# Attention and two feed-forward layers on one core: keys split before they are transposed, GpSimd's long subtractions in parts, column sums as two more columns, weights decoded in place, reciprocals taken through DRAM

## The chip, the cores and the metric

The kernel runs on one core of one Trainium2 chip. The metric is the device time in microseconds of one execution. TensorE (PE) multiplies matrices, VectorE (DVE), ScalarE (ACT) and GpSimd (POOL) work on elements, and SyncE (SP) has the queue from which most DMAs are issued. Every engine takes its instructions strictly in the order in which they were written. GpSimd cannot read PSUM, the memory that matmuls write.

## The reference

The inputs `q`, `k`, `v` have 4 batches, 8 heads, 1152 positions and 64 features. The weights come as float64 and are read as pairs of 32-bit words.

```
q_pool = q.reshape(B, H, S // 2, 2, D).mean(axis=3)
scores = scale * (q_pool @ k.T);  scores -= scores.max(-1)
attn = exp(scores);  attn /= attn.sum(-1) + 1e-9
x = (attn @ v) as rows of 512                    # 2304 tokens
r = maximum(x @ w_in, 0);  y = (s * r * r + b) @ w_out          # d_ff 2048
out = (sigmoid(y @ w_gate) * (y @ w_val)) @ w_out2              # d_ff 1536
```

## The kernel before, in words

**Precision by two parts.** Each float32 operand of a matmul is split into a rounded part ("hi", dtype float32r) and the rest ("lo"), and the product is two or three float32r matmuls (`mm3`, lines 523 to 525: hi by hi, hi by lo, lo by hi). So every operand needs one rounding copy and one subtraction. `copy_sb` (lines 450 and 452) rounds on ACT or POOL, `tt_sb` (line 460) subtracts on DVE or POOL; `copy_ps` (line 457, ACT) and `tt_dve` (line 463, DVE) are used where the source is in PSUM.

**Order.** Nothing is issued where it is written. Each operation is added to a `Plan` with a cost for each engine that may do it, a rank, and its operands. `Plan.order` then plays the whole program through with these costs, gives every operation an engine and a place, and the instructions are issued in that order. `MOVED` holds a shift of rank and of position for each operation's name; `ROOM` says how many buffers a tag has. On DVE, operations marked `port` are not started by the plan while GpSimd works, since the plan takes it that the two share a port.

**Stages.** The 4 batches of attention are worked by pairs of heads (4 a batch, 16 in all). `pair_prep` loads q, k and v of a pair, splits v, adds the two halves of q, transposes q and k by TensorE and splits them on the way out of PSUM. Batch 0 (`pair_rows`) works in rows of queries. Batches 1 to 3 (`pair_half`, `half_head_sums`) work in halves of 288 queries for each head: scores (line 752), copies and a running maximum (457, 463), maximum by transposes (765, 769, 730), subtraction (463), exponential (778), the split `split_p` into `pp` (450, 460), and the product with v (800, 801, 805), which also gives the sums of the exponentials. Then come `sums` (810, with the epsilon), `1 / sums` (822) and `x / sums`. Beside the attention of batch b+1 runs the first feed-forward layer of batch b (`ffn1`). The second layer (`ffn2`) comes after the attention, for two batches at a time, with `ffn1` of batch 3 between.

**The parts that the change touches.** In `pair_prep` the keys of two heads stand side by side in `kn`, nine float32 transposes (686) turn both heads at once, four or one to a PSUM bank, and from each bank go two rounding copies on ACT (457, `kT`) and two subtractions on DVE (463, `kT`), each of 64 partitions. In `decode` a tile of 512 float64 values (`raw`, two buffers) becomes a float32 tile: the high word is limited into `dg` (481, DVE or POOL) and scaled (484, ACT), the low word shifted into `du` (485, DVE), and both joined by two operations (488 and 491, DVE); then `w hi` (450) and `w lo` (460) split it. `dg` and `du` have one buffer each. Batch 0 of `ffn1` decodes its weights and stores the split form to DRAM; later batches fetch that form by POOL's DMA queue (505). The bias b needs the column sums of w_out: in batch 0 eight matmuls with two columns of ones (613) follow each first-half product of four blocks. `split_g` splits the activations of both layers (`g`, `h`).

Of the kernel before, what the change touches and what calls it, by code (L numbers as in the profile page):

```python
# [38 lines left out]
    "q load": (-40, -122),  # L39
    "k load": (-5, -76),  # L40
    "v load": (44, 80),
    "v hi": (-12.5, -104),
    "v lo": (0, 12),
    "q add": (-28.5, 49),
    "q twice": (22, -83),
    "pr qT": (0, 83),
    "pr q hi False": (4.5, 33),
    "pr q lo False": (8, 30),
    "pr q hi True": (0, -76),
    "pr q lo True": (10, -85),  # L50
    "pr kT": (0, 17),
    "pr k hi": (-38.5, 40),
    "pr k lo": (-13, 67),
    "s b load": (0, -46),
    "r qk 1": (0, 238),
    "r max": (30, 219),
    "r - max": (-32, 31),
    "r exp": (21.5, -10),
    "r pT": (-18.5, -7),
    "r p": (-8, 9),  # L60
    "r p hi": (-2.5, -73),
    "r p lo": (-24.5, 146),
    "r pv": (-21, 58),
    "r pT hi": (-7, 104),
    "r pT lo": (44, 48),
    "r o": (-27.5, -23),
    "r x add": (52, -90),
    "r qk 2": (-1, -9),
    "r sums": (-8, -48),
    "r sums eps": (-24, -76),  # L70
    "r 1 / sums": (-9, -19),
    "r spread": (-22, -73),
    "r rows": (-1.5, -88),
    "r rows mid": (0, 341),
    "r x / sums": (0, -15),
    "r x / sums mid": (39, 38),
    "r end": (9.5, 29),
    "ps qT": (0, -24),
    "ps q hi False": (25.5, -60),
    "ps q lo False": (6, 36),  # L80
    "ps kT": (-0.5, -14),
    "ps k hi": (0, -132),
    "ps k lo": (-7, -33),
    "xx hi": (0, 74),
    "xx lo": (-12, -44),
    "w load": (-30, -37),
    "w top": (0, -2),
    "w scale": (-5.5, -17),
    "w low": (-13, -15),
    "w join": (-25.5, -49),  # L90
    "w sign": (-16, 89),
    "w hi": (-40, 12),
    "w lo": (-33.5, -64),
    "w keep": (-21, -47),
    "ff xx up": (46.5, -84),
    "ff relu": (0, 11),
    "square": (-30.5, -41),
    "g hi": (-1, -52),
    "g lo": (-32.5, -66),
    "ff down": (24, -66),  # L100
    "column sums": (58.5, -82),
    "column sum": (42, 14),
    "ff y": (-0.5, 39),
    "ff y add": (7.5, -20),
    "bias": (23, -78),
    "y bias": (19.5, -63),
    "y store": (-40, -99),
    "qk": (-3, -4),
    "s copy": (0, 41),
    "s max": (-0.5, 5),  # L110
    "max T": (0, -4),
    "max": (46.5, 5),
    "max rows": (13, -116),
    "s - max": (9.5, -46),
    "exp": (12.5, 16),
    "p hi": (-33.5, -85),
    "p lo": (51.5, -18),
    "pv hi": (13.5, -11),
    "pv lo": (20.5, 90),
    "sums": (14, 71),  # L120
    "x": (42.5, -28),
    "1 / sums": (60, 83),
    "x / sums": (11.5, -116),
    "w fetch": (42.5, -51),
    "w come": (-31, 87),
    "x store": (0, -158),
    "turn": (0, -29),
    "yy load": (-3, 83),
    "yy hi": (16, -21),
    "yy lo": (3, 111),  # L130
    "p2 yy up": (60, 26),
    "gate": (-30, 45),
    "gate val": (-5, 35),
    "h hi": (30, -36),
    "h lo": (28, 88),
    "down 2": (-36, 27),
    "out": (-11, 22),
    "out add": (5.5, 54),
    "out store": (-24, 145),
    "xx load": (59, -89),  # L140
    "p2 xx up": (-1.5, 27),
    "p2 relu": (0, 42),
    "p2 down": (0, -67),
    "p2 y": (-11.5, -107),
    "p2 y add": (0, 78),
# [196 lines left out]
def kernel(  # L342
# [21 lines left out]
    P = 128  # L364
# [23 lines left out]
    ones = const.tile([P, 1], F32, name="ones")  # L388
    nc.gpsimd.memset(ones, 1.0)
    zero = const.tile([P, 1], F32, name="zero")  # L390
    nc.gpsimd.memset(zero, 0.0)
# [3 lines left out]
    eps = const.tile([P, 1], F32, name="eps")  # L395
    nc.gpsimd.memset(eps, 1e-9)
    ones2 = const.tile([P, 2], F32R, name="ones2")
    nc.vector.tensor_copy(out=ones2, in_=ones.to_broadcast([P, 2]))

    sums2 = const.tile([P, KC], F32, name="sums2")  # L400
    bias = const.tile([P, KC], F32, name="bias")
    s_sb = const.tile([P, 1], F32, name="s_sb")
# [56 lines left out]
    def tt_sb(name, n, out, in0, in1, op, r, w, rank):  # L459
        shared(name, n, lambda e: ENGINE[e].tensor_tensor(out=out(), in0=in0(), in1=in1(), op=op), r, w, rank, 2.15)  # L460
# [3 lines left out]

    def dma(name, n_bytes, issue, r, w, rank):
        plan.add(name, "SP", max(n_bytes / 360.0, 500), issue, r, w, rank)


    def decode(src, w, gate, rank):
        raw = slot("dec", "raw", [P, 512, 2], U32)  # L470
        g = slot("dec", "dg", [P, 512], F32)
        u = slot("dec", "du", [P, 512], U32)
# [626 lines left out]
```

## Time and profile before

| what | value |
|---|---|
| median of 3 runs | 1485.54 us (1484.94 to 1489.52) |
| the profiled execution's own time | 1490.57 us |
| its span, first to last instruction | 1488.8 us |
| mean granted TensorE clock | 0.981 of full speed |
| busy: PE / DVE / ACT / POOL | 1411.6 / 1111.9 / 946.2 / 667.6 us |

The span is that of the profiled execution. Busy time of an engine is time in which it has at least one instruction running. Matmuls overlap each other, so the mean duration of one is longer than the step from one to the next, and the step is read from start times.

### The profile page before, as it was taken

The page shows a single profiled execution, that of the slowest core. Times are in us where ns is not written, and L with a number is a line of the kernel's source. Part 1 is how long each engine was busy: PE and PEld are TensorE (multiplying, and loading weights), DVE is VectorE, ACT ScalarE, POOL GpSimd, SP SyncE. Part 2 cuts the span into 40 slices and gives each one's busy share as a digit, 9 for nine tenths or more (in the row PEclk, how much of TensorE's full clock was granted, in tenths as well). Part 3 has the DMA queues.
Part 4 walks back from the last instruction along what each step waited for, and adds up shares of the span by engine and source line. Part 5 has one row for each costly group of instructions (what it writes and reads, how often), then busy time and mean ns, then how long its engine had stood idle before and what let it go on. Part 6 is the DMA issues. An engine that isn't in the chain of part 4 may idle for free.

```text
span 1488.8 us, 26268 instructions
## 1 busy us (share of the span) xinstructions
PE 1411.6 (95%) x9868; PEld 1346.4 (90%) x9868; DVE 1111.9 (75%) x1848; ACT 946.2 (64%) x2030; POOL 667.6 (45%) x555
## 2 busy tenths in 40 slices
PE   7998899897979999999999999999999999999998
PEld 6887789897869999999999999989998999989897
DVE  6899898889998988888998867667674125757562
ACT  6889888868777989779889965434241524434140
POOL 3666465646575666547766635312222002313120
PEclk9999999899989999999999999999999999999999
DMA  3234313342532513323250335433234543333122
GB/s 88 77 117 155 105 57 106 122 145 94 179 112 82 177 35 144 125 68 103 74 190 24 130 141 204 163 99 99 72 100 121 184 170 100 100 96 103 58 71 64
DMA packets 98510, 165.79 MB, mean 111 GB/s; under 512 B 41936, under 2 KB 75728, under 8 KB 89296
## 3 DMA queue, kind: packets, MB, share of 16 engines
q1 hardware_dynamic: 91472, 113.79, 24.8%
q0 software_dynamic: 6912, 50.33, 9.5%
q8 instruction: 77, 1.26, 0.3%
q14 instruction: 49, 0.40, 0.1%
HBM read 137.89 MB, written 26.21 MB: 110 GB/s over the span
## 4 chain that ended last, share of the span: by engine, by line
PE 73%; DVE 11%; ACT 10%; issue 4%; POOL 1%; DMA 0%; DVEq 0%; ACTq 0%; POOLq 0%
PE banks L523 14%; PE banks L525 14%; PE banks L524 14%; PE banks L752 5%; PE banks L1000 3%; PE banks L1001 3%; PE banks L1002 3%; PE banks L800 3%; PE banks L801 3%; DVE mx L463 3%; PE banks L805 3%; PE banks L920 2%; ACT st L457 2%; PE banks L853 2%; ACT kT L457 2%
## 5 line engine op out<-in xcount | busy, mean ns | idle before, releaser
L525 PE MATMUL banks<-yy,w 128*128 128x288 f32 x768 | 226.4, 295 | 0.0
L524 PE MATMUL banks<-yy,w 128*128 128x288 f32 x768 | 226.2, 294 | 0.0
L523 PE MATMUL banks<-yy,w 128*128 128x288 f32 x768 | 226.0, 294 | 0.0
L460 POOL TENSOR_TENSOR pp<-st,pp 128x864 fp32r<-128x864 f32 x96 | 203.7, 2131 | 36.6 <-ACT pp L450 25.0
L457 ACT COPY st<-banks 128x288 f32<-128x288 f32 x432 | 154.0, 412 | 42.7 <-PE banks L752 31.0
L463 DVE TENSOR_TENSOR mx<-banks,mx 128x288 f32<-128x288 f32 x336 | 151.1, 451 | 27.3 <-ACT st L457 15.1
L752 PE MATMUL banks<-qT,kT 128*128 128x288 f32 x864 | 162.0, 308 | 6.0 <-DVE mx L463 3.8
L523 PE MATMUL banks<-xx,w 128*128 128x288 f32 x512 | 154.5, 302 | 1.6 <-ACT r L593 1.2
L524 PE MATMUL banks<-xx,w 128*128 128x288 f32 x512 | 151.1, 295 | 0.6 <-POOL xx L460 0.6
L525 PE MATMUL banks<-xx,w 128*128 128x288 f32 x512 | 151.0, 295 | 0.0
L463 DVE TENSOR_TENSOR st<-st,banks 128x864 f32<-128x864 f32 x144 | 146.5, 1042 | 5.0 <-PE banks L730 5.0
L778 ACT ACTIVATE st<-st 128x864 f32<-128x864 f32 x144 | 133.4, 936 | 24.2 <-DVE st L463 23.2
L450 ACT CAST w<-du 128x512 fp32r<-128x512 f32 x100 | 62.2, 622 | 132.6 <-DVE du L491 91.2
L523 PEld LDWEIGHTS banks<-yy,w 128*128 128x128 f32 x768 | 144.1, 188 | 0.3
L524 PEld LDWEIGHTS banks<-yy,w 128*128 128x128 f32 x768 | 144.0, 188 | 0.3
L525 PEld LDWEIGHTS banks<-yy,w 128*128 128x128 f32 x768 | 144.0, 188 | 0.0
L752 PEld LDWEIGHTS banks<-qT,kT 128*128 128x128 f32 x864 | 132.1, 195 | 11.3 <-DVE mx L463 6.6
L523 PE MATMUL banks<-g,w 128*128 128x288 f32 x448 | 138.6, 309 | 2.0 <-DVE mx L463 1.4
L800 PE MATMUL banks<-pp,vt 128*128 128x288 f32 x432 | 124.7, 308 | 10.6 <-ACT pp L450 7.5
L525 PE MATMUL banks<-g,w 128*128 128x288 f32 x448 | 133.1, 297 | 0.0
L524 PE MATMUL banks<-g,w 128*128 128x288 f32 x448 | 133.0, 297 | 0.0
L801 PE MATMUL banks<-pp,vt 128*64 128x288 f32 x432 | 121.4, 301 | 0.0
(147 smaller groups left out, 3895.6 us busy)
## 6 DMA issues: line engine op xcount, KB each, us to landing
w<-d_1u_1u POOLq DMA_DIRECT2D x24, 1024.0 KB, 6.1
w<-d_1d_1d POOLq DMA_DIRECT2D x24, 1024.0 KB, 6.2
raw<-in_moe_w_out_dram SPq DMA_DIRECT2D x40, 512.0 KB, 3.4
raw<-in_moe_w_gate_dram SPq DMA_DIRECT2D x24, 512.0 KB, 3.6
raw<-in_moe_w_val_dram SPq DMA_DIRECT2D x24, 512.0 KB, 3.5
qn<-in_q_dram SPq DMA_DIRECT2D x16, 576.0 KB, 4.5
kn<-in_k_dram SPq DMA_DIRECT2D x32, 288.0 KB, 4.1
vn<-in_v_dram SPq DMA_DIRECT2D x32, 288.0 KB, 2.8
```

What stands on the lines that cost most here:

```text
L450: nc.scalar.copy(out=out(), in_=in_())
L457: act(name, n, lambda: nc.scalar.copy(out=out(), in_=in_()), r, w, rank, sbuf=False)
L460: shared(name, n, lambda e: ENGINE[e].tensor_tensor(out=out(), in0=in0(), in1=in1(), op=op), r, w, rank, 2.15)
L463: dve(name, n, lambda: nc.vector.tensor_tensor(out=out(), in0=in0(), in1=in1(), op=op), r, w, rank)
L523: nc.tensor.matmul(ps(), lhsT=whi(), rhs=xhi(), start=first, stop=False)
L524: nc.tensor.matmul(ps(), lhsT=whi(), rhs=xlo(), start=False, stop=False)
L525: nc.tensor.matmul(ps(), lhsT=wlo(), rhs=xhi(), start=False, stop=last)
L752: nc.tensor.matmul(ps.t[:, :HQ], lhsT=kT.t[:, c], rhs=qq[:, w, hf * HQ:(hf + 1) * HQ], start=(w == 0), stop=(w == 1))
L778: act("exp", 3 * HQ, lambda s=s: nc.scalar.activation(out=s.t, in_=s.t, func=AF.Exp), [], parts, AT)
L800: nc.tensor.matmul(acc.t[:, :HQ], lhsT=vt.t[:, 3 * i + c, D:], rhs=hi.t[:, c], start=(i == c == 0), stop=False)
L801: nc.tensor.matmul(acc.t[:D, :HQ], lhsT=vt.t[:, 3 * i + c, :D], rhs=hi.t[:, c], start=False, stop=False)
L805: nc.tensor.matmul(acc.t[:, :HQ], lhsT=vt.t[:, 3 * i + c, D:], rhs=lo.t[:, c], start=False, stop=(i == c == 2))
```

## The change

Five things are changed, and with them the shifts in `MOVED` of nearly every operation and the buffers in `ROOM`.

1. Keys: each head's keys are loaded into a buffer of their own, rounded by `copy_sb` and subtracted by `tt_sb` in their own layout (576 values a partition), so that hi and lo of a head stand side by side in `ks` (one buffer). Nine plain float32r matmuls with a rounded identity then transpose hi and lo of one head together, and one copy (`out_ps`, ACT or DVE) of 128 partitions takes each bank out.
2. GpSimd's part of the subtractions of `pp` is issued as three instructions of 288 values, that of `g` and `h` as two.
3. Column sums: in batch 0, `g` has two more columns (one in hi, zero in lo, written by GpSimd), and the second half's product runs over 290 columns.
4. Decode: every step works on the words of `raw` in place, at a step of two words; `dg` and `du` are gone, `raw` has three buffers. The plan's cost of the limiting step on GpSimd goes from 3.66 to 1.08 ns a value.
5. Reciprocals: for 14 of the 24 halves of a pair (7 of 8 in batch 1, 7 of 8 in batch 2) only one row of the sums for each head leaves PSUM; it goes to DRAM, comes back as 64 by 9, is inverted, goes to DRAM again and comes back spread over 128 partitions. These are five DMAs on SP's queue, each waiting for the step before.

```diff
-    w=4, raw=2, dg=1, du=1, xy=2, xx=1, r=2, g=4,
-    qn=1, kn=1, vn=1, qT=2, kT=2, vt=2, st=6, pp=6,
-    sg=2, mx=3, mc=2, r3=2, ts=1, r9=2, x=1, o=2, s=2,
+    w=4, raw=3, xy=2, xx=1, r=2, g=4,
+    qn=1, kn=2, ks=1, vn=1, qT=2, kT=2, vt=2, st=6, pp=6,
+    sg=2, mx=2, mc=2, r9=1, x=1, s=2, rs=1, rr=1,
...
+    def out_ps(name, n, out, in_, r, w, rank):
+        def issue(e):
+            if e == "ACT":
+                nc.scalar.copy(out=out(), in_=in_())
+            else:
+                nc.vector.tensor_copy(out=out(), in_=in_())
+        plan.add(name, {"ACT": 50 + 0.833 * n, "DVE": 70 + 1.04 * n}, 0, issue, r, w, rank)
...
+            if e == "POOL" and split:
+                for i in range(split):
+                    cut = slice(i * o.shape[1] // split, (i + 1) * o.shape[1] // split)
+                    nc.gpsimd.tensor_tensor(out=o[:, cut], in0=a[:, cut], in1=b[:, cut], op=op)
...
+        low, top = (raw, 0), (raw, 1)
+        def words(i):
+            return raw.t[:, :, i]
...
         shared("w top", 512, lambda e: ENGINE[e].tensor_scalar(
-            out=g.t, in0=raw.t[:, :, 1].bitcast(F32), scalar1=F64_TOP, scalar2=-F64_TOP, op0=ALU.min, op1=ALU.max,
-        ), [raw], [g], rank, 3.66, fast=True)
+            out=words(1).bitcast(F32), in0=words(1).bitcast(F32), scalar1=F64_TOP, scalar2=-F64_TOP, op0=ALU.min, op1=ALU.max,
+        ), [], [top], rank, 1.08, fast=True)
...
         dve("w join", 512, lambda: nc.vector.scalar_tensor_tensor(
-            out=u.t, in0=g.t.bitcast(U32), scalar=3, in1=u.t, op0=ALU.logical_shift_left, op1=ALU.bitwise_or,
-        ), [g], [u], rank, port=True)
+            out=words(0), in0=words(1), scalar=3, in1=words(0), op0=ALU.logical_shift_left, op1=ALU.bitwise_or,
+        ), [top], [low], rank, port=True)
...
+                    n = HQ + 2 if b == 0 and hf else HQ
+                    cs = slice(hf * HQ, hf * HQ + n)
...
-                            for i in range(CH):
-                                for w in range(2):
-                                    nc.tensor.matmul(py.t[:, HQ:HQ + 2], lhsT=w2[i].t[:, w, ds_], rhs=ones2,
-                                                     start=(i == w == 0), stop=(i == CH - 1 and w == 1))
...
+            t = slot("ld", "ks", [P, NK, 2, D], F32R)
+            copy_sb("k hi", NK * D, lambda t=t: t.t[:, :, 0], lambda kn=kn: kn.t, [kn], [(t, 0)], AT)
+            tt_sb("k lo", NK * D, lambda t=t: t.t[:, :, 1], lambda kn=kn: kn.t, lambda t=t: t.t[:, :, 0].bitcast(F32),
+                  ALU.subtract, [kn, (t, 0)], [(t, 1)], AT)
...
-                copy_ps(f"{tag} k hi", n * P, lambda j=j, c0=c0, n=n, lo=lo: kT[j].t[lo, c0:c0 + n], view,
-                        [pt], [(kT[j], 0, c0)], AT)
-                tt_dve(f"{tag} k lo", n * P, lambda j=j, c0=c0, n=n, hi=hi: kT[j].t[hi, c0:c0 + n], view,
-                       lambda j=j, c0=c0, n=n, lo=lo: kT[j].t[lo, c0:c0 + n].bitcast(F32), ALU.subtract,
-                       [pt, (kT[j], 0, c0)], [(kT[j], 1, c0)], AT)
+                def turn_k(j=j, c0=c0, n=n, pt=pt):
+                    for i in range(n):
+                        nc.tensor.matmul(pt.t[:, i * P:(i + 1) * P], lhsT=ks[j].t[:, c0 + i].rearrange("p w d -> p (w d)"),
+                                         rhs=ident_r, start=True, stop=True)
...
+        last = b == B - 1 or hp == NP - 1 and hf == 1
...
+        if last:
+            dve("1 / sums", HQ * 6, lambda: nc.vector.reciprocal(out=sums.t, in_=sums.t), [], both, SK)
+            inv = sums
+        else:
+            inv, both = inverse(sums, both)
```

The new function `inverse` issues, in this order, `sums out`, `sums in`, `1 / sums spread` (DVE, 64 by 9), `1 / sums out` and `1 / sums in` (two DMAs).

## Rows read from the trace of the kernel before

**Rows 1.** Four stages: length, busy us (instructions) of PE, weight loads, DVE, ACT, POOL, clock, DMA share, GB/s.
```profile
0.00:190.00 190.00, 161.47 (x1073) 146.77 (x1074) 160.29 (x346) 158.50 (x454) 105.51 (x126) 0.96 0.35 106
190.00:490.00 300.00, 266.75 (x1871) 255.10 (x1871) 268.26 (x423) 234.41 (x472) 182.00 (x129) 0.93 0.34 111
490.00:857.00 367.00, 357.49 (x2675) 345.35 (x2673) 324.95 (x521) 315.78 (x661) 229.47 (x171) 1.00 0.34 108
857.00:1153.80 296.80, 296.80 (x2010) 283.59 (x2008) 189.83 (x291) 118.57 (x222) 89.05 (x75) 1.00 0.38 125
```

**Rows 2.** The column sums' matmuls alone in one stage (columns as before, PE and weight loads).
```profile
190.00:490.00 300.00, 14.36 (x112) 14.58 (x112) 0.93 0.34 111
```

**Rows 3.** Timeline of PE: start us, us; column sums, key transposes, float32 matmuls.
```profile
255.36 1.84 PE L613 MATMUL banks<-ones,w 128*128 128x2 f32 x16
257.06 0.51 PE L752 MATMUL banks<-qT,kT 128*128 128x288 f32 x2
...
812.85 0.60 PE L686 MATMUL banks<-ident,kn 128*128 128x128 f32 x4
813.20 0.38 PE L523 MATMUL banks<-xx,w 128*128 128x288 f32 x1
813.42 0.30 PE L524 MATMUL banks<-xx,w 128*128 128x288 f32 x1
813.55 0.29 PE L525 MATMUL banks<-xx,w 128*128 128x288 f32 x1
...
76.54 0.33 PE L900 MATMUL banks<-ident,st 128*128 128x64 f32 x2
76.71 0.39 PE L898 MATMUL banks<-ident,st 128*128 128x128 f32 x2
```

**Rows 4.** The key transposes' matmuls alone, by three stages (PE busy, count, weight loads).
```profile
0.00:190.00 190.00, 7.08 (x45) 6.06 (x45) 0.96 0.35 106
490.00:857.00 367.00, 9.65 (x63) 7.49 (x63) 1.00 0.34 108
```

**Rows 5.** Groups in 190 to 490 us: busy us, mean ns, idle before and its releaser.
```profile
L488 DVE SCALAR_TENSOR_TENSOR du<-dg,du 128x512 uint32<-128x512 uint32 x23 | 25.2, 1098 | 0.1
L460 DVE TENSOR_TENSOR pp<-st,pp 128x864 fp32r<-128x864 f32 x15 | 23.8, 1594 | 1.8 <-ACT pp L450 1.5
L491 DVE SCALAR_TENSOR_TENSOR du<-dg,du 128x512 uint32<-128x512 uint32 x23 | 22.4, 975 | 0.0
L485 DVE TENSOR_SCALAR du<-raw 128x512 uint32<-128x512 uint32 x23 | 19.6, 850 | 0.9 <-POOL w L460 0.8
L822 DVE RECIPROCAL s<-s 128x288 f32<-128x288 f32 x8 | 15.6, 1945 | 2.9 <-ACT s L810 2.9
L460 POOL TENSOR_TENSOR pp<-st,pp 128x864 fp32r<-128x864 f32 x37 | 80.1, 2174 | 15.1 <-ACT pp L450 10.2 <-PE banks L805 2.2 <-issue 1.6
```

**Rows 6.** Single durations over the whole kernel, ns: least/median/most.
```profile
L485 DVE TENSOR_SCALAR du<-raw x104: 362/427/2322, 74.1 to 1442.5; 128x512 uint32<-128x512 uint32 x104
L488 DVE SCALAR_TENSOR_TENSOR du<-dg,du x104: 673/692/3122, 75.1 to 1442.9; 128x512 uint32<-128x512 uint32 x104
L460 DVE TENSOR_TENSOR pp<-st,pp x48: 1041/1304/2331, 205.6 to 874.8; 128x864 fp32r<-128x864 f32 x48
L460 DVE TENSOR_TENSOR vt<-vn,vt x8: 749/759/2127, 267.6 to 842.1; 128x576 fp32r<-128x576 f32 x8
```

**Rows 7.** DVE's groups over the whole kernel: keys, and the small reciprocal.
```profile
L463 DVE TENSOR_TENSOR kT<-banks,kT 64x512 fp32r<-64x512 f32 x64 | 44.1, 689 | 9.6 <-ACT kT L457 7.1 <-PE banks L525 1.3
L463 DVE TENSOR_TENSOR kT<-banks,kT 64x128 fp32r<-64x128 f32 x32 | 9.3, 289 | 1.1 <-ACT kT L457 0.3
L943 DVE RECIPROCAL r<-r 128x9 f32<-128x9 f32 x4 | 0.8, 203 | 0.0
```

**Rows 8.** DMA issues, a small store: KB, median us from issue to landing.
```profile
x_d<-x SPq DMA_DIRECT2D x8, 144.0 KB, 1.7
```

**Rows 9.** Waits of SP's queue, the largest group: us in total, times, longest.
```profile
SPq L476 <- DVE du L485: 355.8, 50, 90.2
```

More of the change, by code (lines that the diff above doesn't have):

```diff
@@ L57 @@
[L57 to L145, printed above, removed]
+    "q load": (0, -58),
+    "k load": (0, -101),
+    "k hi": (0, 2),
+    "k lo": (0, 110),
+    "v load": (51, -86),
+    "v hi": (6, -69),
+    "v lo": (-39.5, -11),
+    "q add": (-2.5, -102),
@@ new lines @@
+    "q twice": (60, 40),
+    "pr qT": (-7, -53),
+    "pr q hi False": (0, -40),
+    "pr q lo False": (-23.5, 107),
+    "pr q hi True": (-10, 61),
+    "pr q lo True": (0, 70),
+    "pr kT": (2, 13),
+    "pr k out": (-32, -40),
+    "s b load": (0, -88),
+    "r qk 1": (24.5, -53),
+    "r max": (51.5, -91),
+    "r - max": (-34.5, 126),
+    "r exp": (56, -48),
+    "r pT": (-40, 99),
+    "r p": (-17.5, -122),
+    "r p hi": (-0.5, -87),
+    "r p lo": (-19.5, 107),
+    "r pv": (-1, -26),
@@ new lines @@
+    "r pT hi": (-15, -119),
+    "r pT lo": (57, -31),
+    "r o": (-33.5, -85),
+    "r x add": (59.5, -99),
+    "r qk 2": (0, 5),
+    "r sums": (-17, 38),
+    "r sums eps": (0, -84),
+    "r 1 / sums": (0, -54),
+    "r spread": (-40, 67),
+    "r rows": (0, 46),
+    "r rows mid": (32.5, 5),
+    "r x / sums": (-5.5, 96),
+    "r x / sums mid": (0, -31),
+    "r end": (0, 156),
+    "ps qT": (1, -44),
+    "ps q hi False": (41.5, -91),
+    "ps q lo False": (0, 68),
+    "ps kT": (-1, -34),
@@ new lines @@
+    "ps k out": (0, 41),
+    "xx hi": (-8, -110),
+    "xx lo": (0, -65),
+    "w load": (-17, -4),
+    "w top": (39, -71),
+    "w scale": (-1.5, -116),
+    "w low": (1, 120),
+    "w join": (-33, -86),
+    "w sign": (0.5, 29),
+    "w hi": (-18, 15),
+    "w lo": (-39.5, 34),
+    "w keep": (-1.5, -101),
+    "one": (10.5, 50),
+    "ff xx up": (45, 58),
+    "ff relu": (1, 15),
+    "square": (0, -110),
+    "g hi": (-8.5, -93),
+    "g lo": (-32.5, -3),
+    "ff down": (1.5, -21),
+    "ff y": (-1.5, -80),
@@ new lines @@
+    "column sum": (4, -20),
+    "ff y add": (2.5, -106),
+    "bias": (-18.5, -20),
+    "y bias": (29.5, 20),
+    "y store": (23.5, -89),
+    "qk": (-4.5, 21),
+    "s copy": (19, -100),
+    "s max": (2.5, 77),
+    "max T": (-37, 8),
+    "max": (58, -40),
+    "max rows": (-2.5, -69),
+    "s - max": (13, -15),
+    "exp": (1, -126),
+    "p hi": (-40, -170),
+    "p lo": (47, -19),
+    "pv hi": (0.5, -58),
+    "pv lo": (0, -2),
+    "sums": (23.5, -3),
+    "x": (53, -165),
+    "sums out": (27, -26),
@@ new lines @@
+    "sums in": (0, -92),
+    "1 / sums spread": (-40, 54),
+    "1 / sums out": (8, 104),
+    "1 / sums in": (0, 42),
+    "x / sums": (44.5, 2),
+    "1 / sums": (28, 40),
+    "w fetch": (21.5, 79),
+    "w come": (31.5, -29),
+    "x store": (-40, -69),
+    "turn": (0, -59),
+    "yy load": (22, 38),
+    "yy hi": (58, 75),
+    "yy lo": (-20.5, 25),
+    "p2 yy up": (33, -3),
+    "gate": (20, 45),
+    "gate val": (-9, 90),
+    "h hi": (1.5, -76),
+    "h lo": (0, -37),
+    "down 2": (-13.5, -75),
@@ L146 @@
+    "out": (0, 93),
+    "out add": (60, 4),
+    "out store": (-13, 88),
+    "xx load": (0, -104),
+    "p2 xx up": (0, -10),
+    "p2 relu": (0, 35),
+    "p2 down": (2, -1),
+    "p2 y": (-40, 6),
+    "p2 y add": (17.5, 23),
 }
@@ L498, in weights @@
+        copy_sb("w hi", 512, lambda: w.t[:, 0, :], lambda: words(0).bitcast(F32), [low], [(w, 0)], rank)
+        tt_sb("w lo", 512, lambda: w.t[:, 1, :], lambda: words(0).bitcast(F32), lambda: w.t[:, 0, :].bitcast(F32), ALU.subtract,
+              [low, (w, 0)], [(w, 1)], rank)
     def weights(pair, gate=(), rank=FE, keep=False, kept=False):
@@ L585, in ffn1 @@
                 else:
-                    gg = slot("fg", "g", [P, 2, SQ], F32R)
+                    gg = slot("fg", "g", [P, 2, SQ + 2], F32R)
+                if b == 0:
+                    plan.add("one", "POOL", 150, lambda gg=gg: nc.gpsimd.tensor_scalar(
+                        out=gg.t[:, :, SQ:], in0=one_zero.bitcast(F32), scalar1=1.0, scalar2=0.0, op0=ALU.mult, op1=ALU.add),
+                             [], [(gg, "one")], FE)
                 both = [(r, 0), (r, 1)]
```

133 lines of the change are left out of this document (67 added, 66 removed).

## The prediction

> **What bounds the kernel now.** I read the busy times by stage first. From 857 us on TensorE is busy without a gap for almost 300 us while DVE, ACT and POOL have much time left, and the rest is of the same kind [rows 1]. The change does little on TensorE there, so that part cannot move by much. Between 490 and 857 us TensorE is busy 357.5 of 367 us at full clock, so only 9.5 us are left to win, and every matmul added costs its time. The two stages before are different. In 0 to 190 us TensorE is idle 28.5 us and in 190 to 490 us 33.3 us, and its mean granted clock is 0.96 and 0.93, which is the lower of its two levels, 1.2 GHz, for part of the time after such gaps (at that level it does half the work, so 1 minus 0.93, times 300, or 21 us, are lost in the second stage and 7.6 us in the first) [rows 1]. In 190 to 490 us DVE is the busiest engine, 268.3 of 300 us, ACT has 234.4 and POOL 182.0 [rows 1].
>
> Next I looked at what DVE does there. Many of its instructions take far longer than the same form usually does: the shift of the low word 850 ns against a median of 427, the join 1098 against 692, the subtraction of `pp` 1594 against 1304 [rows 5, 6]. They stand in DVE's busy time, but part of it is waiting. The cause that the rows offer is GpSimd's long subtractions, 37 in this stage of 2174 ns each [rows 5]. The longest DVE shift takes 2322 ns, about one such subtraction and a shift [rows 5, 6].
>
> **The change part by part**, in the profiled execution's own time, 1490.6 us (5 us above the median of the runs shown).
>
> *Reciprocals.* A large one takes 1945 ns [rows 5], the small one that stands in its place I put at 203 ns, the time of a 128 by 9 one [rows 7]. Seven fall away in 190 to 490 us: 7 times 1.742 is 12.2 us of DVE; seven more fall away later in the same way. The price is latency. Each trip has four legs over DRAM; at 1.7 us for a small store [rows 8] that is about 7 us until `x / sums` can run. Hidden, I take it, since x is needed only when a whole batch is done and the batch's last half keeps the old way. What queues behind a waiting leg is SP's queue; that is a rival below.
>
> *Keys on DVE.* Before, a pair costs 4 times 0.689 and 2 times 0.289, or 3.33 us of DVE [rows 7]. After, DVE may get two subtractions of 576 values at 0.749 us (the least for v's, the same shape) [rows 6] and six copies out of PSUM, which I take as at most the subtractions out of PSUM that they replace, 3.33 us in all. Either may go to another engine. If DVE gets none, a pair saves 3.3 us; if all, it costs 1.5 us more. I take half: 0.75 plus 1.67, a saving of 0.9 us a pair. Four pairs in the second stage make 3.7 us. ACT, which copied six banks before, copies as much at most, plus its part of the roundings.
>
> *Keys on TensorE.* Before, four transposes take 813.42 minus 812.85, less the 0.13 us step of the matmul that follows them, which is 0.44 us, or 0.11 us each; nine make 1.0 us a pair [rows 3]. After, there are 18 float32r matmuls of 128 columns. The trace has none of that size. With two columns each takes 257.06 minus 255.36 over 16, 0.106 us, which only the loading of weights can set; with 288 the step is 0.13 us [rows 3]. I take 0.106, as 128 columns lie nearer to the small end in streaming time: 1.9 us, 0.9 us more a pair. With 0.13 it is 1.4 us more. By stage there are 5 pairs, 4 pairs, and 7 pairs (63 transposes of nine each) [rows 4]: plus 4.6, 3.7 and 6.4 us.
>
> *Column sums.* 112 of them lie in the second stage [rows 2], at 0.106 us 11.9 us of TensorE; 16 more, 1.7 us, right behind. In their place 192 products run over two more columns, at 0.13 us over 288 columns 0.2 us in all. GpSimd's 16 small writes of the two columns have no row; at 0.2 us (a small DVE operation, [rows 7]) they are 3 us on the engine with the most room.
>
> *GpSimd in parts.* The excess over the medians in 190 to 490 us is 23 times 0.406 for the join, 23 times 0.283 for the sign (same form), 23 times 0.423 for the shift and 15 times 0.29 for `pp`: 29.9 us [rows 5, 6]. How much of it is due to the long subtractions? One that meets a running instruction waits half its length on average, so shares go by busy time times length: 80.1 times 2.17 is 174 for `pp`, and POOL's other 101.9 us at some 1.3 us each, an estimate, make 132 [rows 1, 5]. So 57%. Parts a third as long leave a third of that: 38% of 29.9, 11.4 us, is saved. The ends are nothing and 17 us.
>
> This is where a rule can be weighed. The rows show single DVE instructions held up by as much as one GpSimd instruction lasts [rows 6]. The Trainium skill, SBUF — State Buffer, section "SBUF: two separate sides", says that DVE and GpSimd share one pair of ports, and that whoever starts first keeps the pair for its whole instruction while the other is blocked. By that rule the 11.4 us stand. If the pair were shared by bandwidth, cutting the instruction would save nothing, and my total below would be some 6 us worse. The same rule has a side against this change, which is a rival below.
>
> *Decode in place.* The reading side already goes by steps of two words in the shift, with a least time of 362 ns for 512 values, so I see no sign that the step slows it [rows 6]. For the other steps the trace shows no such form: below, nothing is gained; above, if each of the 23 pairs of joins ran at the stage's slow 1.1 us instead of 0.69 [rows 5, 6], 19 us of DVE would come back. I take zero, nearest to the shift's row. Three buffers for raw relieve SP, which waits longest for the release of raw [rows 9], but no row of TensorE shows it waiting for weights, so I count nothing. After 857 us DVE has a third of its time free, which hides it there [rows 1].
>
> *Order.* Every shift in `MOVED` is new. No row prices that; both signs are possible and it is in the range.
>
> **The sum by stage.** Second stage: DVE loses 12.2, 3.7 and 11.4, 27.3 of 268.3 us, 10%. If DVE alone sets its length, 30.5 us go. If DVE sets nothing, TensorE's 11.9 less 0.2 less 3.7 leaves 8 us. I take the middle, 19 us, because idle and lost clock (54 us together) leave room for it, but ACT at 78% comes next. First stage: DVE loses 4.6 of 160.3 us, worth at most 5.4 us; TensorE gains 4.6 us of work, and the first pair's keys pass two more steps before they can be transposed. I take minus 1. Third stage: TensorE gains 6.4 less 1.7, 4.7 us; DVE's relief by 12.2 and 6.3 us may fill some of the 9.5 us of idle, I take 3 us. Plus 2. Together minus 18: 1472.6 for a profiled execution like this one, **1467 us** beside the median of 1485.5.
>
> **The rivals.**
> *More is won* (0.13). DVE sets the whole second stage and, with fewer gaps, half of the lost clock returns: 30.5, 5.4 and 14 less, 2 more: about 1438 us. For it: DVE at 89%. Against: TensorE's last waits in single places are short, and the work of each engine is chained with the others.
> *Only TensorE's part counts* (0.10). ACT or the order sets the early stages: minus 8, plus 4.6, plus 4.7, so 1486 us, no change.
> *128 columns cost as float32 does* (0.08). One float32 product of 64 columns is two instructions and takes 76.71 minus 76.54, 0.17 us [rows 3]; two weight loads for 128 columns would be 0.21 us. Then 288 products take 30 us more than I count: 1497 us. It decides when one takes over 0.17 us. Against it: float32r products of 288 columns take 0.13.
> *SP's queue is held by the round trips* (0.05), the case of a loss by waits: three legs of 1.7 us keep SP 5 us, fourteen times, and loads of keys, values or weights wait behind. If TensorE loses 3 us each time, 42 us: 1509 us. It decides from 1.3 us each (18 over 14). Against it: loads are issued early, and SP already spends 356 us waiting for one kind of release alone [rows 9].
> *GpSimd falls behind* (0.06). Three parts must each get the ports, so DVE can step in twice more. Of the 144 subtractions of `pp` (three for each head of 24 halves) DVE had 48 [rows 6], so GpSimd 96. At half a join, 0.35 us each time, they lose 67 us of POOL's time, and the product with `pp`'s rest waits for them. If a third of it reaches TensorE, 22 us: 1489 us. This is what the skill's rule above would do if DVE always stood ready. Against it: POOL is busy only 61% of the second stage [rows 1].
>
> **How the numbers follow.** My forecast has 0.58, with 1452 to 1480 as its own range. A measurement tells 0.3%, 4.5 us, from no change. The forecast, the larger gain and 0.02 of the case of TensorE alone are faster: 0.73. The rest of that case (0.08) and 0.02 each of the last products' and GpSimd's cases are within 0.3%: 0.12. Slower is 0.06, 0.05 and 0.04: 0.15. The range goes from 1438 to 1492: it leaves out half of the larger gain, SP's case and most of the float32 case, under 0.2.
>
> **What would show it.** In the profile after: idle and clock of the stage to 490 us better, its length near 280 us; the shift's and join's means near their medians; 14 reciprocals of about 0.2 us; `pp` on POOL as three of about 0.7 us; the key products 0.11 us apart; the stage that TensorE fills as long as before or a few us longer. I would be wrong if DVE's busy share stayed near 0.89 in a stage just as long, if strided joins took over 0.8 us each, or if TensorE waited on keys or values behind SP.

## The result, and the profile after

The changed kernel takes 1473.35 us (median; 1472.27 to 1475.20) beside 1487.37 us for the kernel before on the same chip, a ratio of 0.9908, with a 95% interval of 0.9885 to 0.9930. It is 14 us faster; 18 were forecast. The profiled execution takes 1472.71 us, with a span of 1470.9 us and a mean granted clock of 0.989.

The stages first: after, length, then busy us (instructions) of PE, weight loads, DVE, ACT, POOL, clock, DMA share, GB/s.

```profile
0.00:190.00 190.00, 163.02 (x1122) 149.48 (x1123) 152.97 (x337) 157.05 (x454) 127.07 (x144) 0.98 0.35 108
190.00:490.00 300.00, 276.20 (x1960) 263.19 (x1959) 244.91 (x425) 251.83 (x510) 249.28 (x271) 0.96 0.39 130
490.00:857.00 367.00, 363.13 (x2737) 354.62 (x2735) 302.45 (x509) 315.53 (x646) 263.30 (x292) 1.00 0.33 109
857.00:1153.80 296.80, 293.16 (x1962) 277.54 (x1961) 173.94 (x247) 108.97 (x201) 113.92 (x110) 1.00 0.39 128
```

Against [rows 1], TensorE's idle time in the second stage falls from 33.3 to 23.8 us and its clock rises from 0.93 to 0.96. DVE falls to 0.82 of that stage. What was not forecast is POOL: 249.28 us instead of 182.00, now as full as DVE and ACT. The page's list of busy times and its last chain say the same.

```profile
PE 1407.7 (96%) x9884; PEld 1342.2 (91%) x9884; DVE 1030.8 (70%) x1749; ACT 939.6 (64%) x2003; POOL 847.2 (58%) x908
...
PE 69%; POOL 13%; ACT 6%; DMA 4%; DVE 4%; issue 4%; SPq 0%; POOLq 0%; DVEq 0%; ACTq 0%
```

POOL has 180 us more work than before (667.6), DVE 81 less. The largest shares over the whole kernel are GpSimd's subtractions of `pp` (60 us more), the limiting step, which GpSimd now does for all 104 tiles instead of 52 (49 us more), the splitting of the weights (113.2 instead of 68.3 us) and the splitting of the keys, which is new there (51.2 us). Two of these groups before, then after (busy us, mean ns, idle before and its releaser):

```profile
L460 POOL TENSOR_TENSOR pp<-st,pp 128x864 fp32r<-128x864 f32 x96 | 203.7, 2131 | 36.6 <-ACT pp L450 25.0 <-PE banks L525 4.5 <-PE banks L805 2.4
L481 POOL TENSOR_SCALAR dg<-raw 128x512 f32<-128x512 f32 x52 | 35.3, 680 | 167.5 <-DVE du L491 125.8 <-issue 21.2 <-ACT r L591 4.6
...
L482 POOL TENSOR_TENSOR pp<-st,pp 128x288 fp32r<-128x288 f32 x303 | 264.1, 902 | 29.3 <-ACT pp L456 27.5
L510 POOL TENSOR_SCALAR raw<-raw 128x512 f32<-128x512 f32 x104 | 84.3, 815 | 129.2 <-DMA raw<-in_moe_w_val_dram 50.6 <-DMA raw<-in_moe_w_gate_dram 34.2 <-DMA raw<-in_moe_w_out_dram 22.6
```

Which POOL instruction stands in the chain is seen in the groups of the second stage (busy us, mean ns, idle before it and its releaser) and in TensorE's largest wait of the whole kernel (us in total, times, longest).

```profile
L482 POOL TENSOR_TENSOR pp<-st,pp 128x288 fp32r<-128x288 f32 x132 | 118.4, 927 | 5.3 <-ACT pp L456 4.8
L840 PE MATMUL banks<-pp,vt 128*128 128x288 f32 x168 | 39.7, 324 | 12.3 <-POOL pp L482 12.3
L520 DVE SCALAR_TENSOR_TENSOR raw<-raw 128x512 uint32<-128x512 uint32 x21 | 20.3, 968 | 0.0
L517 DVE SCALAR_TENSOR_TENSOR raw<-raw 128x512 uint32<-128x512 uint32 x21 | 19.7, 940 | 1.7 <-ACT raw L513 1.6
...
PE banks L840 <- POOL pp L482: 14.8, 29, 2.1
```

Line 482 is GpSimd's subtraction of `pp`, now three instructions (132 are 44 subtractions), and line 840 is the product that needs the result. Three parts take 2.69 us (118.4 over 44) where one whole subtraction took 2.17 [rows 5]. The joins of the decode (517 and 520) are still far above their medians over the whole kernel, 694 and 688 ns.

The smaller steps can be read from single rows: four key products in TensorE's timeline (start us, us) and three groups over the whole kernel.

```profile
779.89 0.56 PE L754 MATMUL banks<-ident_r,ks 128*128 128x128 f32 x4
780.29 0.35 PE L552 MATMUL banks<-xx,w 128*128 128x288 f32 x1
780.47 0.30 PE L553 MATMUL banks<-xx,w 128*128 128x288 f32 x1
```

```profile
L864 DVE RECIPROCAL rs<-rs 64x9 f32<-64x9 f32 x14 | 2.8, 198 | 0.7 <-DMA rs<-s_d 0.7
L617 POOL TENSOR_SCALAR g<-one_zero 128x4 fp32r<-128x4 f32 x16 | 2.9, 205 | 3.9 <-PE banks L985 2.0 <-DVE mx L489 1.7
L513 ACT ACTIVATE raw<-raw 128x512 f32<-128x512 f32 x104 | 71.3, 689 | 97.1 <-POOL raw L510 96.7
```

Read as in the prediction, four key products take 780.47 minus 779.89 less 0.13, 0.45 us or 0.11 each. The small reciprocal and the writing of the two columns cost what was put down for them.

### The profile page after: what moved, and what is told of

Its sections match the earlier page's. It is cut to its first block, busy times and chain, and to the rows that moved or that the text cites. A ratio compares the mean times of both kernels' runs of the same rounds, so it can differ in the third digit from the quotient of the medians.

```text
span 1470.9 us, 26672 instructions
## 1 busy us (share of the span) xinstructions
PE 1407.7 (96%) x9884; PEld 1342.2 (91%) x9884; DVE 1030.8 (70%) x1749; ACT 939.6 (64%) x2003; POOL 847.2 (58%) x908
## 4 chain that ended last, share of the span: by engine, by line
PE 69%; POOL 13%; ACT 6%; DMA 4%; DVE 4%; issue 4%; SPq 0%; POOLq 0%; DVEq 0%; ACTq 0%
PE banks L552 13%; PE banks L554 13%; PE banks L553 13%; POOL pp L482 7%; PE banks L787 4%; PE banks L1067 3%; PE banks L1066 3%; PE banks L1065 3%; PE banks L840 2%; PE banks L835 2%; PE banks L836 2%; PE banks L985 2%; PE banks L918 1%; PE banks L754 1%; PE banks L963 1%
## 5 line engine op out<-in xcount | busy, mean ns | idle before, releaser
L482 POOL TENSOR_TENSOR pp<-st,pp 128x288 fp32r<-128x288 f32 x303 | 264.1, 902 | 29.3 <-ACT pp L456 27.5
L510 POOL TENSOR_SCALAR raw<-raw 128x512 f32<-128x512 f32 x104 | 84.3, 815 | 129.2 <-DMA raw<-in_moe_w_val_dram 50.6
L552 PE MATMUL banks<-g,w 128*128 128x288 f32 x448 | 135.2, 302 | 1.2 <-ACT xy L463 1.2
L513 ACT ACTIVATE raw<-raw 128x512 f32<-128x512 f32 x104 | 71.3, 689 | 97.1 <-POOL raw L510 96.7
L787 PEld LDWEIGHTS banks<-qT,kT 128*128 128x128 f32 x864 | 129.1, 191 | 4.5 <-ACT st L463 1.5
L553 PE MATMUL banks<-g,w 128*128 128x288 f32 x448 | 132.7, 296 | 0.0
L554 PE MATMUL banks<-g,w 128*128 128x288 f32 x448 | 132.6, 296 | 0.0
```

The costliest lines, as they stand in the source:

```text
L482: nc.gpsimd.tensor_tensor(out=o[:, cut], in0=a[:, cut], in1=b[:, cut], op=op)
L510: shared("w top", 512, lambda e: ENGINE[e].tensor_scalar(out=words(1).bitcast(F32), in0=words(1).bitcast(F32), scalar1=F64_TOP, scalar2=-F ...
L513: act("w scale", 512, lambda: nc.scalar.mul(words(1).bitcast(F32), words(1).bitcast(F32), 2.0 ** -112), [], [top], rank)
L552: nc.tensor.matmul(ps(), lhsT=whi(), rhs=xhi(), start=first, stop=False)
L553: nc.tensor.matmul(ps(), lhsT=whi(), rhs=xlo(), start=False, stop=False)
L554: nc.tensor.matmul(ps(), lhsT=wlo(), rhs=xhi(), start=False, stop=last)
```

## The experiments

Where a run has "the order kept", the plan sees the same operations with the same costs, so every other instruction keeps its place and engine. Changes are given against the changed kernel's 1473.35 us, or as a ratio to the kernel before.

**Whole subtractions, order kept.** GpSimd's subtractions are undone alone.

```diff
-            if e == "POOL" and split:
+            if e == "POOL" and split > 9:
```

> The changed kernel, in the same order on every engine, with GpSimd's subtractions of pp, g and h issued whole again (864 and 576 values). Theory A, that the parts free DVE: the shift and the joins wait longer again in 190 to 490 us (means back towards 1.1 us for the join), DVE loses some 11 us there, the kernel takes 5 to 8 us more, about 1479 us. Theory B, that the parts cost GpSimd more than they free: in the changed kernel's trace a part of pp takes 902 ns, three take 2.7 us, where a whole one took 2.1; 101 subtractions of pp then lose some 60 us of GpSimd's time, TensorE waits 15 us in all for the last part, and the whole form is faster than the changed kernel by 5 to 12 us, about 1465 us.

1464.94 us (1463.51 to 1465.65), ratio 0.9858 [0.9841, 0.9876]: 8.4 us faster than with the parts, theory B. (The run with the tiles 64 bytes lower, below, keeps the parts; measured beside this one on the same chip it took 1473.34 us.) The same groups of the second stage, the page's busy times and its chain:

```profile
L484 POOL TENSOR_TENSOR pp<-st,pp 128x864 fp32r<-128x864 f32 x44 | 98.5, 2248 | 6.2 <-ACT pp L456 5.0 <-POOL g L484 0.8
L840 PE MATMUL banks<-pp,vt 128*128 128x288 f32 x168 | 34.6, 315 | 8.3 <-POOL pp L484 8.3
L520 DVE SCALAR_TENSOR_TENSOR raw<-raw 128x512 uint32<-128x512 uint32 x21 | 25.8, 1228 | 0.0
L517 DVE SCALAR_TENSOR_TENSOR raw<-raw 128x512 uint32<-128x512 uint32 x21 | 23.9, 1137 | 0.8 <-ACT raw L513 0.7
```

```profile
PE 1405.9 (96%) x9884; PEld 1343.6 (92%) x9884; DVE 1065.9 (73%) x1749; ACT 939.5 (64%) x2003; POOL 797.9 (55%) x667
...
PE 75%; ACT 9%; DVE 6%; POOL 3%; issue 3%; DMA 3%; DVEq 0%; SPq 0%; POOLq 0%; ACTq 0%
```

The parts do free DVE: without them the joins are 0.2 to 0.26 us longer each, and DVE has 35.1 us more. But GpSimd has 49.3 us less, TensorE's wait for `pp` in this stage falls from 12.3 to 8.3 us, and POOL's share of the chain from 13 to 3%. So the parts shortened the waits on DVE and paid for it with time on GpSimd, for which TensorE was waiting.

**Whole subtractions and small copies, order kept.** GpSimd pays for more instructions, DVE gets no relief.

```diff
+                if e == "POOL" and split:
+                    for i in range(3 if split == 3 else 1):
+                        nc.gpsimd.tensor_scalar(out=scratch[:, :2], in0=b[:, 0, :2] if len(b.shape) == 3 else b[:, :2], ...)
                 ENGINE[e].tensor_tensor(out=o, in0=a, in1=b, op=op)
```

> The changed kernel with its order kept and GpSimd's subtractions whole, as in the run with whole subtractions (1465 us), but ahead of each whole subtraction of pp GpSimd issues three small copies of two columns (about 0.2 us each), ahead of each of g and h one; they wait for the same operands and nobody reads what they write. So GpSimd pays about what the parts cost it (some 60 us), and DVE keeps the long waits for whole subtractions. Theory A, it is GpSimd's time that the parts cost TensorE: the 8 us come back and more, since DVE gets no relief for it, 1474 to 1485 us. Theory B, the parts lose for another reason, such as DVE stepping in between two of them: 1465 to 1468 us.

1510.44 us (1507.18 to 1511.75), ratio 1.0154 [1.0125, 1.0182]: 45.5 us more than without the copies; theory A had the direction, but neither had the size. A group of the whole kernel and TensorE's largest wait:

```profile
L487 POOL TENSOR_SCALAR scratch<-pp 128x2 f32<-128x2 f32 x303 | 77.6, 256 | 46.7 <-ACT pp L457 28.0
```

```profile
PE banks L844 <- POOL pp L488: 37.7, 42, 4.3
```

POOL's busy time rises by 72.8 us (870.7 on its page, 797.9 without the copies), and most of the loss stands in this one wait: 37.7 us, where the run without the copies shows 8.3. So GpSimd's time ahead of line 840 is what TensorE pays for. By this run's rate, 45.5 us for 72.8, the 49.3 us that the parts cost GpSimd would be about 31 us, and DVE's relief would have given back some 22 of them. This is an estimate, since the copies stand in another place than the parts; the run with nine reciprocals below, 13 us for 23.1 us of DVE, makes about 20 of the 35.1 us.

**Parts alone in the kernel before, its own order.** The changed `tt_sb` is put into the kernel before, three parts for `pp`, two for `g` and `h`.

```diff
-        tt_sb("p lo", 3 * HQ, ..., ALU.subtract, [*parts, hi], [lo], SK)
+        tt_sb("p lo", 3 * HQ, ..., ALU.subtract, [*parts, hi], [lo], SK, 3)
```

> The kernel before, in its own order, with only GpSimd's subtractions in parts (pp in three, g and h in two). Theory A, parts free DVE and DVE sets the stage: as my sum had it, about 6 us less, 1480 us. Theory B, from the run with whole subtractions: three parts cost GpSimd 0.6 us more than a whole one, 96 times, 56 us; but GpSimd is less busy in the kernel before (182 of 300 us in the second stage, not 249), so less of it reaches TensorE than the 8 us lost in the changed kernel: 2 to 6 us more, about 1490 us.

1489.08 us, ratio 1.0021 [1.0005, 1.0036]: 2 to 3 us slower, theory B. DVE's busy time falls from 1111.9 to 1073.3 us, in the second stage from 268.26 to 253.17, and POOL's rises from 667.6 to 726.3. The parts don't pay here either, though POOL has more room in this kernel [rows 1].

```profile
190.00:490.00 300.00, 268.61 (x1894) 255.95 (x1894) 253.17 (x431) 237.32 (x477) 206.79 (x219) 0.94 0.36 118
...
PE 1404.8 (95%) x9868; PEld 1336.7 (90%) x9868; DVE 1073.3 (72%) x1848; ACT 945.3 (64%) x2030; POOL 726.3 (49%) x806
```

**Nine small reciprocals instead of one, order kept.**

```diff
-        dve("1 / sums spread", 54, lambda: nc.vector.reciprocal(out=rs.t, in_=rs.t), [], [rs], SK)
+        dve("1 / sums spread", 54, nine, [], [rs], SK)      # nine: the same instruction nine times
```

> The changed kernel, in the same order, with the small reciprocal (64 by 9) done nine times in its place, so that DVE gets back 14 times 8 times 0.198, 22 us of work, and the trip through DRAM stays (nine times gives 1/x again). Theory A, that DVE's relief by the reciprocals is what pays: 7 of the 14 lie where TensorE still waits, and the kernel takes 6 to 10 us more, about 1481 us. Theory B, that GpSimd is now the engine that sets that stage: under 3 us more, about 1475 us.

1486.38 us, ratio 1.0010 [0.9995, 1.0026]: 13 us slower than the change, somewhat over theory A. The 112 instructions more are 23.1 us of DVE at 206 ns, about what the change took away. In this order more than half of DVE's added time reaches the end. (They also make each trip through DRAM 1.6 us longer; that this costs nothing is taken, not shown.)

**Short reciprocals in the kernel before, its own order.**

```diff
-        dve("1 / sums", HQ * 6, lambda: nc.vector.reciprocal(out=sums.t, in_=sums.t), ...)
+        dve("1 / sums", HQ * 6, invert, ...)    # 14 of 24: nc.vector.reciprocal(out=sums.t[:, :16], in_=sums.t[:, :16])
```

> The kernel before in its own order, where the 14 large reciprocals that the change takes through DRAM invert only 16 of 288 columns (the inverses of the others are left out), so DVE loses about 14 times 1.74, 24.4 us, and nothing is put on another engine or queue. Theory A, DVE's relief is worth here what it was worth in the changed kernel (13 us): 1474 us, a ratio of 0.991. Theory B, the kernel before hides more of it, as the sum of the prediction had it (about 0.6 of it in the second stage, little later): minus 7 to 10, 1478 to 1480 us, a ratio of 0.994. Theory C, hidden: no change.

1484.81 us, ratio 0.9988 [0.9973, 1.0003]: hidden, theory C. The view of the second stage, a group of it, and two of TensorE's waits in it before, then in this run:

```profile
190.00:490.00 300.00, 267.29 (x1887) 255.58 (x1887) 258.86 (x430) 236.81 (x474) 182.37 (x129) 0.94 0.35 113
```

```profile
L800 PE MATMUL banks<-pp,vt 128*128 128x288 f32 x156 | 47.6, 322 | 12.9 <-ACT pp L450 9.5 <-POOL pp L452 1.9 <-ACT r L591 1.5
```

```profile
PE banks L800 <- ACT pp L450: 7.5, 1, 7.5
PE banks L730 <- DVE mc L769: 4.9, 2, 3.8
...
PE banks L800 <- ACT pp L450: 9.5, 3, 7.5
PE banks L730 <- DVE mc L769: 3.5, 2, 2.5
```

DVE's time in the stage falls from 268.26 to 258.86 us, and TensorE does the same work (267.29 for 266.75). TensorE's waits for DVE become a little shorter, but line 800's wait for ACT's rounding of `pp` grows; most of it is one wait of 7.5 us, which stands before as well. So DVE, the busiest engine of this stage [rows 1], did not alone set its length in the kernel before.

**Column sums put back, order kept.** The 128 small matmuls run as before; nobody reads their result.

```diff
+                        for i in range(CH):
+                            for w in range(2):
+                                nc.tensor.matmul(py.t[:, HQ + 12:HQ + 14], lhsT=w2[i].t[:, w, ds_], rhs=one_zero[:, 0], ...)
```

> The changed kernel, in the same order, with the 128 small matmuls for column sums put back behind the products of 290 columns, their result unused. At 0.106 us each they are 13.6 us of TensorE. If all of it lies on the path: 1487 us, all of the change's gain. If the gaps of TensorE there hide it: no change, 1473 us. My sum counted 8 to 12 us: about 1483 us.

1483.25 us, ratio 0.9985 [0.9969, 1.0000]: 10 us slower for 128 times 0.106, 13.6 us of TensorE.

**Key products twice, order kept.**

```diff
+                        for _ in range(2):
                             nc.tensor.matmul(pt.t[:, i * P:(i + 1) * P], lhsT=ks[j].t[:, c0 + i]..., rhs=ident_r, start=True, stop=True)
```

> The changed kernel with its order kept, each of the 288 key products issued twice into the same place, so TensorE has 288 times 0.11, 31.7 us more, and nothing else changes. Theory A, the keys' work on TensorE stands whole on the path in every stage, so that the 14.6 us by which it grew in the change were paid whole: plus 27 to 32, 1500 to 1505 us. Theory B, TensorE's idle time before 490 us takes much of it: plus 12 to 20, 1485 to 1493 us.

1497.68 us (1494.21 to 1499.14), ratio 1.0068 [1.0044, 1.0092]: 24.3 us for the 31.7 us of TensorE that were put down for it, between the two theories. At that rate, 0.77, the 14.6 us by which the keys grew on TensorE (16 pairs, 0.9 each) would cost about 11 us, an estimate.

**Old keys, old decode, old order, each planned anew.** In three runs the plan was played through again: the changed kernel with the keys transposed and split as before and `MOVED` else unchanged; with `dg`, `du` and two raw buffers as before; and with all of the changed operations but the `MOVED` of before for every name that both have.

> The changed kernel with the old way for keys: nine float32 transposes for two heads, four copies and subtractions out of PSUM; the rest and its shifts stay, the order is planned anew. TensorE does 288 products of 0.11 us less and 144 transposes of 0.11 us more, minus 15 us of work; GpSimd loses 25 subtractions of 1.46 and 19 roundings of 0.78, 51 us; DVE gets 53 us and loses 31. Theory A, that the new keys pay by taking work off DVE and ACT: about 8 us more, 1481 us. Theory B, that their added TensorE and GpSimd work costs as much as it frees: within 4 us of the changed kernel, 1473 us, or faster, if TensorE's 15 us count in full, down to 1462 us.

> The changed kernel with the old decode through dg and du (one buffer each) and two buffers for raw; the price of the limiting step on GpSimd stays 1.08 in the plan, the order is planned anew. My sum counted decode in place at zero: 1473 us. In the trace ACT's scaling takes 689 against 630 ns and GpSimd's w lo a median of 1.50 against 1.30 us in place, some 6 and 12 us of their time: if that counts, 2 to 4 us less, 1470 us. If three buffers in flight are what helps, 3 to 6 us more, 1478 us.

> The changed kernel with the shifts of the kernel before for every operation that has one in both, so that the operations are those of the changed kernel in an order planned with other shifts. If the five edits make the gain whatever the order: within 5 us of 1473 us. If the shifts of the changed kernel carry a part of it: 1480 to 1495 us. The difference also tells how far a newly planned order alone moves the time, which the two runs above have in them.

They take 1546.55 us (ratio 1.0400 [1.0379, 1.0421]), 1522.65 us (1.0236 [1.0216, 1.0257]) and 1526.43 us (1.0258 [1.0233, 1.0282]). The third changes no operation at all and moves the time by 53 us, so the first two tell nothing of keys or decode: a `MOVED` made for one set of operations is worth tens of microseconds to that set and costs as much with another. Only runs with the order kept separate a part.

**Two runs on the step of the last layer's products.** In the trace after, the products over 512 columns of the last layer follow each other in 0.232 to 0.233 us, in the trace before in 0.227. One run lays the changed kernel's tiles 64 bytes lower (two pairs of small constants merged), the other puts an unused constant of 448 bytes into the kernel before, so that its weight tiles lie where they lie after.

```diff
-    sums2 = const.tile([P, KC], F32, name="sums2")
-    bias = const.tile([P, KC], F32, name="bias")
+    small = const.tile([P, 2 * KC], F32, name="small")
+    sums2, bias = small[:, :KC], small[:, KC:]
```

> The changed kernel, in the same order, with two pairs of small constants each in one tile, so that the weights, h and all tiles behind lie 64 bytes lower in SBUF, on multiples of 128 bytes again as in the kernel before. In the changed kernel's trace the 512-column products of the second layer follow each other at 0.234 us, before at 0.226. If the place in memory is the reason: the step goes back to 0.226, 648 of them give 5 us, about 1468 us. If it is not: the step stays and the time too, 1473 us.

> The kernel before in its own order with one unused small constant, which moves the weights' tiles up by 448 bytes to the address that they have in the changed kernel. Theory A, the address of the tiles sets the step of the last layer's products over 512 columns (0.227 us before, 0.232 to 0.233 after): the step goes to 0.232 or more, 3 to 4 us longer, a ratio of 1.002. Theory B, it is not the address: 0.227 and no change.

1473.34 us with the step still at 0.232, and a ratio of 1.0005 [0.9991, 1.0020] with the step at 0.227. So it is not the address. The second run is also a second profile of the kernel before (span 1483.0 us), and serves as that below. Its stages:

```profile
0.00:190.00 190.00, 159.43 (x1096) 143.77 (x1097) 160.90 (x350) 160.46 (x461) 109.13 (x129) 0.99 0.35 106
190.00:490.00 300.00, 267.84 (x1885) 256.32 (x1885) 270.54 (x429) 236.26 (x475) 182.90 (x129) 0.93 0.35 112
490.00:857.00 367.00, 357.40 (x2671) 345.21 (x2670) 324.62 (x518) 315.99 (x662) 230.52 (x171) 1.00 0.34 108
857.00:1153.80 296.80, 296.66 (x2006) 283.36 (x2005) 186.71 (x286) 114.85 (x214) 85.43 (x73) 1.00 0.40 130
```

## Why the prediction was right, and where it was not

**The size and the place.** 1473.35 us lies in the likeliest case's own range, 1452 to 1480. Where the time was won can be read from TensorE's busy time still to come at each boundary: its total (1405.8 us in that second profile, 1407.7 after) less the sums of the stages above. At 190 us the changed kernel is 1.7 us ahead, at 490 us 10.0, at 857 us 15.8, at 1153.8 us 12.3, and its span is 12.1 us shorter. The stages brought 1.7, 8.3, 5.8, a loss of 3.5, and nothing; forecast were 1, 19, a loss of 2, nothing, nothing. Part of the difference between the second and third stage comes from this way of counting: the 4.7 us net that the change adds to TensorE's work in the third stage are still to come at 490 us, so in work common to both kernels the changed one is 14.7 us ahead there, of 20 forecast. The third stage's idle time fell from 9.6 to 3.9 us, by 5.7 where 3 were taken. The loss after 857 us was not forecast. It is idle time: TensorE stands still for 3.6 us there after the change and for 0.1 before, 2.2 of them until a weight tile lands and 1.4 until ACT has rounded `h`. The products over 512 columns that step more slowly all come after 857 us too; 648 times 0.0055 is another 3.6 us, which lies in the work still to come at every boundary up to there.

```profile
L552 PE MATMUL banks<-xx,w 128*128 128x288 f32 x98 | 28.9, 295 | 2.2 <-DMA w<-d_1u_1u 2.2
L1065 PE MATMUL banks<-w,h 128*128 128x512 f32 x108 | 42.7, 396 | 1.4 <-ACT h L456 1.4
```

**The step that failed is "GpSimd in parts".** It counted 11.4 us of DVE as saved and priced nothing on GpSimd; the price stood only in a rival, at 0.06. DVE's saving was there, and larger: 35.1 us over the kernel, 22.3 in the stage from 190 to 490 us (267.22 without parts, 244.91 with), and 15.1 there in the kernel before. But the parts made the changed kernel 8.4 us slower, and the kernel before 2 to 3 us. In the sum of the second stage, which took the middle of DVE's and TensorE's accounts, they stand for half of 11.4, so this one term is off by about 14 us. The room on GpSimd that the prediction pointed to, 61% busy in the second stage, was that of the kernel before; after the other parts of the change it is 79% there without the parts (237.27 us) and 83% with them.

**The other terms were too small together.** Without the parts the changed kernel gains 1486.37 minus 1464.94, 21.4 us, where the sum without that term has 18 less 5.7, 12.3: 9 us too little, against the 14 too much of the parts. That the sum came within 6 us of the measurement is luck, two errors that offset each other. Put back with the order kept, the column sums cost 10 us (about 8 counted: half of 11.9, and 1.7 behind it) and DVE's 23 us of reciprocals 13 us (about 6 in the second stage and part of the 3 in the third). The keys on TensorE cost, by the estimate above, about 11 us against it. These don't add up to a price list. In the kernel before, DVE's relief alone brought under 2 us, within the noise (the run with short reciprocals), and the parts alone a loss. In the changed kernel TensorE's wait for ACT's rounding of `pp` in the second stage is down from 7.5 to 0.9 us; that DVE's relief pays there because the order has moved this wait is a reading that no run shows. What the order, the decode in place, the third raw buffer and the keys' relief of DVE and ACT each bring was not separated: with the order kept the decode's old form was not tried, and another order changes everything at once.

**The rule on the ports.** Line 517's longest join takes 1619 ns with the parts and 2542 ns with whole subtractions, against a median of 694 in both.

```profile
L517 DVE SCALAR_TENSOR_TENSOR raw<-raw x104: 674/694/1619, 98.1 to 1414.9; 128x512 uint32<-128x512 uint32 x104
```

```profile
L517 DVE SCALAR_TENSOR_TENSOR raw<-raw x104: 624/694/2542, 100.0 to 1407.9; 128x512 uint32<-128x512 uint32 x104
```

What each of the long ones stood beside is seen in the timeline: with whole subtractions, then two joins of line 520 in the change (start us, us).

```profile
273.65 2.34 POOL L484 TENSOR_TENSOR pp<-st,pp 128x864 fp32r<-128x864 f32 x1 [0.19 <-ACT pp L456]
274.00 2.54 DVE L517 SCALAR_TENSOR_TENSOR raw<-raw 128x512 uint32<-128x512 uint32 x1
...
139.17 1.43 POOL L484 TENSOR_TENSOR ks<-kn,ks 128x576 fp32r<-128x576 f32 x1
139.31 1.85 DVE L520 SCALAR_TENSOR_TENSOR raw<-raw 128x512 uint32<-128x512 uint32 x1
...
279.20 2.79 POOL L482 TENSOR_TENSOR pp<-st,pp 128x288 fp32r<-128x288 f32 x3
280.00 1.33 DVE L520 SCALAR_TENSOR_TENSOR raw<-raw 128x512 uint32<-128x512 uint32 x1
```

The first join ends 0.55 us after the subtraction of `pp` that was running when it started, the second, the longest of line 520, as much after a subtraction of the keys, which the change does not cut. The longest join beside parts of `pp`, the third, takes 1.33 us. So a join is held until the running GpSimd instruction ends, part or whole; line 517's 1619 ns too stand beside an uncut subtraction, of the weights. This agrees with the Trainium skill, SBUF — State Buffer, section "SBUF: two separate sides", by which one of the two keeps the shared ports for a whole instruction. The mechanism of the step was right; what it left out is that each part is an instruction of its own, with a cost of its own.

**The rivals.** *GpSimd falls behind* (0.06) names the place of the loss, the product that waits for `pp`'s rest, but not its size (8 us net, not 22) and only in part its mechanism, DVE stepping in between two parts. The 101 subtractions of `pp` take 264.1 us in parts and 220.0 whole, 0.44 us more each. But even the quickest three parts in the trace take 2.32 us, and the quickest whole subtraction 2.005, so about 0.3 of the 0.44 us is there where nothing is held up.

```profile
L484 POOL TENSOR_TENSOR pp<-st,pp 128x864 fp32r<-128x864 f32 x101 | 220.0, 2188 | 33.6 <-ACT pp L456 29.6 <-DVE xy L484 1.1 <-POOL g L484 0.8
...
424.30 2.32 POOL L482 TENSOR_TENSOR pp<-st,pp 128x288 fp32r<-128x288 f32 x3
```

*SP's queue held by the round trips*: the legs do wait, 25.2 us in all for the small reciprocal and 17.9 for the next leg, but TensorE's waits name none of them, and its only wait for a weight load is 2.2 us.

```profile
SPq L865 <- DVE rs L864: 25.2, 9, 4.9
SPq L869 <- DMA r_d<-rs: 17.9, 12, 4.0
```

*128 columns at float32's price*: 0.11 us each, as taken. *Only TensorE's part* and *more is won*: neither; DVE's time is worth something in the new order, and TensorE's idle time in the second stage is still 23.8 us.

**Decode in place.** The joins' medians stay at 694 and 688 ns [rows 6], so the step of two words costs DVE nothing, as taken. The prediction named strided joins of over 0.8 us as a sign of being wrong, and their means in the second stage, 0.94 and 0.97 us, are over it; by the medians these are joins held up, not slow ones. The step costs ACT: the scaling takes 689 ns each, 630 before at line 484, 6.1 us over 104 tiles.

**A version faster than both** is the changed kernel with whole subtractions, 1464.94 us.

## What to carry to other kernels

An instruction that is cut up to free another engine must be priced on the engine that is cut: count the instructions added, and ask who waits for the last of them. A busy engine is not yet the one that sets the end; take its load away once, at its place, before a gain is counted from it. In a kernel with an order laid out ahead, test parts with that order kept, since a new one alone moves more than most parts.

## What the runs showed of the hardware

- One GpSimd subtraction of 864 values has a median of 2065 ns, a part of 288 values 809 ns (the two rows below, of whole subtractions and of the change: least/median/most). Neighbouring records overlap by some 40 ns, so three parts in a row are best read from their start to their end: 2.32 us at the quickest, beside 2005 ns, or some 160 ns for each instruction more; in the mean of all, with what holds them up, it is 218 ns (44.1 us over 202 instructions). A GpSimd copy of two columns took 256 ns in the mean. The Trainium skill, GPSIMD Engine Reference, section "2.1 Instruction dispatch", speaks of tens of cycles for one step of starting an instruction; the whole cost seen here is larger.

```profile
L484 POOL TENSOR_TENSOR pp<-st,pp x101: 2005/2065/3064, 204.6 to 828.9; 128x864 fp32r<-128x864 f32 x101
```

```profile
L482 POOL TENSOR_TENSOR pp<-st,pp x303: 787/809/1805, 200.7 to 835.6; 128x288 fp32r<-128x288 f32 x152
```

- The last layer's products over 512 columns step at 0.227 us in every profile with the operations of before and at 0.232 to 0.233 us in every profile with most of the changed ones, whatever the order. Moving the tiles did not change it in either kernel; the cause stays open.
- ACT's scaling of 512 words is 59 ns slower at a step of two words (689 for 630), while DVE's joins do not change (medians of 694 and 688 for 692).
